# An attention decode kernel: a third P buffer with K units mixed into value stages, no dummy transposes, and the last QK of a phase at once

## The chip, the cores and the metric

The kernel runs on one core of one Trainium2 chip. The metric is device time in microseconds of that core. PE is the matrix engine, DVE the vector engine, ACT the scalar engine, SP the engine that here issues all loads. "Granted clock" is the share of PE's full clock that the throttle let through; 0.50 is half speed.

Ratios are the mean time of one kernel's fast runs over the mean of the fast runs of the kernel before in the same rounds on the same chip, so a ratio is not quite the quotient of the medians quoted. A stage length is one execution's.

## The reference, cut to what matters

Two layers, each attention with a KV cache and then a gated feed-forward block, applied twice to four rows (B = 4) of one token each. Both attention layers read the same caches.

```
q = (layernorm(x) @ wq)                     # 32 heads of 128, 8 KV heads: 4 query heads share one
scores = q @ k_cache^T * 128**-0.5          # k_cache, v_cache: (4 rows, 8 groups, 8192, 128), bf16
o = softmax(scores) @ v_cache
x = x + o @ wo
x = x + (silu(layernorm(x) @ w_gate) * (layernorm(x) @ w_up)) @ w_down
# the same once more
```

K and V of one row are 33.6 MB. The kernel keeps eleven value pieces of 512 KB of a row on the chip from the first layer to the second; the rest of the caches is read twice.

## The kernel before

The work is cut into units of 2048 cache positions of one group, 512 KB each. A K unit transposes its 16 blocks on PE, copies them out of PSUM, the memory that PE writes (DVE or ACT), and multiplies with the query (QK). After the eight groups of a chunk comes the softmax; after the fourth chunk a finalization that rescales P and transposes it. A value unit is 16 narrow matmuls of P against V. Between value units the kernel before issues dummy transposes, whose results nothing reads; the function is called `warm`.

```
NRING = 7; NRET = 11; NKT = 6          # load ring, kept value buffers, transposed-K buffers
pp = sb("pp", [P, 2, S // NJ], BF16)   # P of two rows (layer, row) -> row % 2
...
phases = [("A1", 0, A_of(0, 0, range(NCH)))]                       # K of row 0, layer 1
for b in range(B):
    ...                                                             # B1: values of row b, layer 1,
    phases.append(("B1", b, mine))                                  #     merged with K of row b+1; 5 values at the end
    phases.append(("C1", b, fill))                                  # C1: feed-forward + 11 value units of row b+1
    phases.append(("A2", b, merge(A_of(1, b, range(NCH)), mid) + tail))   # A2: K of row b, layer 2
    phases.append(("B2", b, B_of(1, b, gs_)))                       # B2: values of row b, layer 2, alone
...
def do(u):
    if u[0] == "k":
        hv = k_front(u)                           # transposes and copies
        prev, pending[:] = list(pending), [(u, hv)]
        for x in prev:
            k_back(*x)                            # QK of the K unit before this one
    else:
        v_unit(u)
        if last_kind[0] == "v":
            warm(warmth["n"])                     # 8 dummy transposes (4 in C1)
    last_kind[0] = u[0]
    run_delayed()
    pump()                                        # next loads, as ring buffers come free
...
elif name == "B1":
    some(len(units)); flush(); settle()           # the last QK only here, after the value tail
```

I call C1 the feed-forward stage, A2 the second-layer K stage, B2 the second-layer value stage. The last B2 also contains the final feed-forward and the output.

## Time and profile before

| | before |
|---|---|
| time, median (3 runs) | 759.7 us (758.5 to 761.5) |
| profiled span | 764.7 us |
| PE busy / DVE / ACT | 87% / 42% / 31% |
| loads | 259.3 MB, mean 341 GB/s with all packets |

From the page of the kernel before: engines, clock and transfer rate in 40 slices of 19.1 us, the DMA account, the chain that ended last, and two groups of instructions (line, engine, operation, operands, count; then busy us and mean ns of one; then idle time before them).

```profile
span 764.7 us, 28617 instructions
PE 668.4 (87%) x13048; PEld 516.8 (68%) x13048; DVE 324.5 (42%) x727; ACT 235.2 (31%) x304; POOL 0.7 (0%) x6
PEclk9989788995799999996599999997599996699898
GB/s 354 388 390 407 367 404 378 410 409 238 262 402 407 334 278 407 408 408 261 237 381 405 367 288 352 409 408 325 239 337 407 349 328 281 258 406 356 295 256 62
DMA packets 75129, 261.13 MB, mean 341 GB/s; under 512 B 7672, under 2 KB 13568, under 8 KB 74496
PE 62%; DMA 25%; DVE 5%; issue 3%; ACT 3%; SPq 2%; ACTq 0%
L384 PE MATMUL ps<-ident,ring 128*128 128x128 bf16 x4096 | 286.6, 226 | 26.4 <-DMA ring<-in_A_k_cache_dram 26.1
L518 PE MATMUL ps<-ident 128*128 128x128 bf16 x1440 | 129.4, 236 | 0.8 <-issue 0.6
```

The best slices move 407 to 410 GB/s. PE seems the fuller engine, but line 518 are the dummies: 129.4 us of its 668.4. The Trainium skill ("Perfetto Trace Analysis", opening note) says that matmul busy time is a bad metric of nearness to the limit; its reason is that matmuls are pipelined. Here there is another: a fifth of the busy time computes nothing.

The windows view gives one stage per line: from:to, length, busy time of each engine, then granted clock, DMA share and GB/s. I cut within 0.3 us of the first matmul of each stage's first unit. In order: feed-forward of row 0, value stage of row 0, feed-forward of row 1, value stage of row 1, last value stage and output.

```profile
176.40:198.80 22.40, 22.40 (x552) 19.03 (x553) 4.72 (x25) 1.26 (x5) 0.00 (x0) 0.50 0.66 217
255.90:287.40 31.50, 29.76 (x785) 22.76 (x782) 3.85 (x15) 0.00 (x0) 0.00 (x0) 1.00 0.86 293
352.60:375.60 23.00, 22.51 (x553) 19.08 (x553) 4.72 (x25) 1.26 (x5) 0.00 (x0) 0.50 0.66 213
433.50:467.40 33.90, 30.93 (x788) 23.77 (x785) 3.88 (x15) 0.00 (x0) 0.00 (x0) 0.95 0.89 301
720.00:764.70 44.70, 39.22 (x1083) 31.88 (x1082) 7.45 (x33) 0.75 (x3) 0.00 (x0) 0.93 0.56 189
```

The feed-forward stages have PE full at half clock and the queue at 213 to 217 GB/s. The value stages have PE full at full clock (with dummies) and the queue at 293 to 301.

### The profile page before, as it was taken

How to read it: one execution, taken by the hardware profiler on the slowest of the kernel's cores; microseconds unless marked ns; L12 is line 12 of the kernel's file. 1: busy time of each engine (PE TensorE's matmuls, PEld its weight loads, DVE VectorE, ACT ScalarE, POOL GpSimd, SP SyncE). 2: the span in 40 equal slices, each digit the busy share in tenths (PEclk: the TensorE clock that was granted, in tenths of full speed). 3: DMA queues.
4: the chain of work that ended last, by engine and by line, in shares of the span. 5: the costliest groups of instructions: out<-in, count | busy, mean ns of one | idle time of the engine just before them, and what ended most of it. 6: DMA issues, size and time to landing. Idle time of an engine off the chain costs nothing.

```text
span 764.7 us, 28617 instructions
## 1 busy us (share of the span) xinstructions
PE 668.4 (87%) x13048; PEld 516.8 (68%) x13048; DVE 324.5 (42%) x727; ACT 235.2 (31%) x304; POOL 0.7 (0%) x6
## 2 busy tenths in 40 slices
PE   3888678778999998997999999997999899999797
PEld 3655556557876776666877667665877677876576
DVE  2545444433366215544266413653266511366312
ACT  0544233321265004541156102551056300156100
POOL 0000000000000000000000000000000000000000
PEclk9989788995799999996599999997599996699898
DMA  8999999996899989997799989998799887899872
GB/s 354 388 390 407 367 404 378 410 409 238 262 402 407 334 278 407 408 408 261 237 381 405 367 288 352 409 408 325 239 337 407 349 328 281 258 406 356 295 256 62
DMA packets 75129, 261.13 MB, mean 341 GB/s; under 512 B 7672, under 2 KB 13568, under 8 KB 74496
## 3 DMA queue, kind: packets, MB, share of 16 engines
q1 hardware_dynamic: 75008, 259.30, 90.4%
q8 instruction: 102, 1.67, 0.9%
q14 instruction: 19, 0.16, 0.1%
HBM read 259.26 MB, written 0.00 MB: 339 GB/s over the span
## 4 chain that ended last, share of the span: by engine, by line
PE 62%; DMA 25%; DVE 5%; issue 3%; ACT 3%; SPq 2%; ACTq 0%
PE ps L384 22%; DMA ring<-in_A_k_cache_dram 18%; PE ps L518 14%; PE ps L497 10%; PE ps L400 6%; DMA ring<-in_A_v_cache_dram 6%; PE ps L580 2%; SPq L92 2%; PE ps L599 2%; DMA wq_sb<-in_A_wq_dram 2%; PE ps L540 2%; DVE negm L412 1%; ACT ktp L250 1%; PE ps L635 1%; ACT pp L414 1%
## 5 line engine op out<-in xcount | busy, mean ns | idle before, releaser
L384 PE MATMUL ps<-ident,ring 128*128 128x128 bf16 x4096 | 286.6, 226 | 26.4 <-DMA ring<-in_A_k_cache_dram 26.1
L384 PEld LDWEIGHTS ps<-ident,ring 128*128 128x128 bf16 x4096 | 242.8, 101 | 77.8 <-DMA ring<-in_A_k_cache_dram 45.2
L248 DVE COPY ktp<-ps 128x1024 bf16<-128x1024 bf16 x320 | 215.2, 689 | 178.3 <-PE ps L384 177.1
L250 ACT ACTIVATE ktp<-ps 128x1024 bf16<-128x1024 bf16 x192 | 195.1, 1022 | 293.7 <-PE ps L384 293.7
L518 PE MATMUL ps<-ident 128*128 128x128 bf16 x1440 | 129.4, 236 | 0.8 <-issue 0.6
L400 PE MATMUL ps<-ktp,qpad 128*32 128x512 bf16 x1024 | 110.7, 398 | 2.8 <-ACT ktp L250 2.4
L518 PEld LDWEIGHTS ps<-ident 128*128 128x128 bf16 x1440 | 89.4, 104 | 27.5 <-issue 11.6
L497 PE MATMUL ps<-ring,pp 128*32 128x128 bf16 x2688 | 82.3, 251 | 9.7 <-issue 5.0
L506 DVE TENSOR_SCALAR o_g<-ps,wrow 128x128 bf16<-128x128 f32 x64 | 22.4, 349 | 142.3 <-PE ps L497 142.3
L497 PEld LDWEIGHTS ps<-ring,pp 128*32 128x32 bf16 x2688 | 48.7, 107 | 25.7 <-issue 10.3
L400 PEld LDWEIGHTS ps<-ktp,qpad 128*32 128x32 bf16 x1024 | 27.9, 93 | 35.8 <-ACT ktp L250 6.3
L573 ACT ACTIVATE lnv<-var,eps_sb 128x4 f32<-128x4 f32 x10 | 3.0, 298 | 156.4 <-DVE var L560 156.4
L497 PE MATMUL ps<-kept,pp 128*32 128x128 bf16 x1408 | 36.7, 223 | 6.3 <-DMA kept<-in_A_v_cache_dram 4.4
L414 ACT ACTIVATE pp<-ps,negm 128x512 bf16<-128x512 f32 x32 | 22.0, 687 | 44.9 <-DVE negm L412 42.7
L497 PEld LDWEIGHTS ps<-kept,pp 128*32 128x32 bf16 x1408 | 22.0, 96 | 14.0 <-DMA kept<-in_A_v_cache_dram 6.5
L412 DVE TENSOR_REDUCE negm<-ps 128x1 f32<-128x512 f32 x32 | 22.1, 690 | 7.7 <-PE ps L400 6.0
L580 PE MATMUL ps<-xnT,wq_sb 128*128 128x4 bf16 x640 | 17.9, 166 | 8.3 <-DMA wq_sb<-in_A_wq_dram 7.8
L540 PEld LDWEIGHTS ps<-oT,wo_sb 128*128 128x128 bf16 x640 | 20.2, 99 | 7.0 <-issue 4.2
L540 PE MATMUL ps<-oT,wo_sb 128*128 128x4 bf16 x640 | 22.2, 165 | 2.5 <-DVE oT L528 1.3
L580 PEld LDWEIGHTS ps<-xnT,wq_sb 128*128 128x128 bf16 x640 | 17.6, 104 | 8.5 <-DMA wq_sb<-in_A_wq_dram 7.9
L447 PE MATMUL ps<-ident,pp 128*128 128x128 bf16 x128 | 10.9, 244 | 10.6 <-DVE pp L431 10.6
L525 PE MATMUL ps<-selh,o_g 128*128 128x4 bf16 x64 | 11.6, 180 | 9.0 <-DVE o_g L506 8.6
(76 smaller groups left out, 195.4 us busy)
## 6 DMA issues: line engine op xcount, KB each, us to landing
ring<-in_A_k_cache_dram SPq DMA_DIRECT2D x256, 512.0 KB, 7.2
ring<-in_A_v_cache_dram SPq DMA_DIRECT2D x168, 512.0 KB, 6.8
kept<-in_A_v_cache_dram SPq DMA_DIRECT2D x44, 512.0 KB, 9.9
wq_sb<-in_A_wq_dram SPq DMA_DIRECT2D x1, 4096.0 KB, 12.5
wo_sb<-in_A_wo_dram SPq DMA_DIRECT2D x4, 1024.0 KB, 12.0
wg_sb<-in_B_w_gate_dram SPq DMA_DIRECT2D x2, 896.0 KB, 12.0
wu_sb<-in_B_w_up_dram SPq DMA_DIRECT2D x2, 896.0 KB, 11.9
wd_sb<-in_B_w_down_dram SPq DMA_DIRECT2D x2, 896.0 KB, 9.3
```

What stands on the lines that cost most here:

```text
L92: ins = self.eng[engname].dma_start(out_ap, in_ap)
L248: T.op("dve", lambda e: e.tensor_copy(dst, src), reads=reads, writes=writes)
L250: T.op("act", lambda e: e.activation(dst, src, ACTF.Copy), reads=reads, writes=writes)
L384: T.op("pe", lambda e: e.matmul(stg[:, t * P:(t + 1) * P], lhsT=ap[:, blk * Dh:(blk + 1) * Dh], rhs=ident[:], is_transpose=True, start=Tru ...
L400: T.op("pe", lambda e: e.matmul(ps[32 * j:32 * (j + 1), bk * BW:(bk + 1) * BW], lhsT=qp, rhs=ktp[:, s, (j % 2) * 512:(j % 2 + 1) * 512], s ...
L412: T.op("dve", lambda e: e.tensor_reduce(negm[:, q, c:c + 1], bank(bk), AX.X, ALU.max, negate=True), reads=[f"pb{bk}"], writes=[f"negm{q}_{ ...
L414: T.op("act", lambda e: e.activation(pp[:, q, c * 512:(c + 1) * 512], bank(bk), ACTF.Exp, bias=negm[:, q, c:c + 1], scale=1.0, accum_out=l ...
L497: T.op("pe", lambda e: e.matmul(ps[32 * j:32 * (j + 1), bk * BW:bk * BW + Dh], lhsT=pp[:, q, (c * NM + m) * P + 32 * j:(c * NM + m) * P + ...
L506: T.op("dve", lambda e: e.tensor_scalar(o_g[:, og, :], ps[:, bk * BW:bk * BW + Dh], wrow[:, q:q + 1], None, op0=ALU.mult), reads=[f"pb{bk} ...
L518: T.op("pe", lambda e: e.matmul(stg[:, 0:P], lhsT=ident[:], rhs=ident[:], is_transpose=True, start=True, stop=True), reads=["ident"], writ ...
L540: T.op("pe", lambda e: e.matmul(ps[:, OPJ * BW + nq * B:OPJ * BW + (nq + 1) * B], lhsT=wo_sb[:, h, nq * P:(nq + 1) * P], rhs=oT[:, l, h, : ...
L580: T.op("pe", lambda e: e.matmul(misc[:, h * B:(h + 1) * B], lhsT=wq_sb[:, kt, h * Dh:(h + 1) * Dh], rhs=xnT[:, kt * B:(kt + 1) * B], start ...
```

## The change

Its intent: with P buffers for three rows, the K units of the next-but-one row can run in the second-layer value stage, where they bring loads into stretches that only use kept values. Value units are redistributed over feed-forward and K stages. The dummy transposes go. The last QK of a first-layer phase is issued at once, as that of a second-layer phase was before, so that the softmax and the transposes of P run behind the value units at the end of the phase. To pay for the third P buffer, six transposed-K buffers become four. The core of the diff (the code for alternating PSUM banks, `ALT`, is added but switched off):

```diff
-    NKT = 6
+    NKT = 4
...
-        pp = sb("pp", [P, 2, S // NJ], BF16)
+        pp = sb("pp", [P, 3, S // NJ], BF16)
...
+        TAIL1 = [16, 7, 8]
+        TAIL2 = [3, 4, 3, 4]
+        NFILL = [10, 13, 14, 9]
+        LATE = [8, 8, 16]
...
+            v2, late = split(B_of(1, b, V2O[b]), (LATE + [0])[b])
+            if b + 1 < B:
+                v2 = v2 + B_of(0, b + 1, V1O[b + 1][5:])
+            if b + 2 < B:
+                early = B_of(0, b + 2, V1O[b + 2][:5])
+                head, tail = split(v2, TAIL1[b + 1])
+                v2 = head[:LEAD[b]] + mix(A_of(0, b + 2, range(NCH)), head[LEAD[b]:]) + tail
...
-            pbuf[(0, b)] = b % 2
-            pbuf[(1, b)] = b % 2
+            pbuf[(0, b)] = b % 3
+            pbuf[(1, b)] = b % 3
...
             if u[0] == "k":
                 hv = k_front(u)
-                prev, pending[:] = list(pending), [(u, hv)]
-                for x in prev:
-                    k_back(*x)
+                if not hold["on"]:
+                    flush()
+                pending.append((u, hv))
+                if u[3] == G - 1 and u[4] == NCH - 1:
+                    flush()
             else:
                 v_unit(u)
-                if last_kind[0] == "v":
-                    warm(warmth["n"])
...
```

More of the change, by code (lines that the diff above doesn't have):

```diff
@@ L167, in bass_interleave_layers__gqa_block_cached__swiglu_ffn__decode_kernel @@
         xnT = sb("xnT", [P, NQ * B], BF16)
-        negm = sb("negm", [P, 2, NCH], FP32)
-        lsum = sb("lsum", [P, 2, NCH], FP32)
-        gm = sb("gm", [P, 2, 2], FP32)
+        negm = sb("negm", [P, 3, NCH], FP32)
+        lsum = sb("lsum", [P, 3, NCH], FP32)
+        gm = sb("gm", [P, 3, 2], FP32)
         dm = sb("dm", [P, NCH], FP32)
-        alpha = sb("alpha", [P, 2, NCH], FP32)
+        alpha = sb("alpha", [P, 3, NCH], FP32)
         wl = sb("wl", [P, NCH], FP32)
@@ L178, in bass_interleave_layers__gqa_block_cached__swiglu_ffn__decode_kernel @@
         one1 = sb("one1", [1, 1], FP32)
-        wrow = sb("wrow", [P, 2], FP32)
+        wrow = sb("wrow", [P, 3], FP32)
         o_g = sb("o_g", [P, 2, Dh], BF16)
@@ L198, in bass_interleave_layers__gqa_block_cached__swiglu_ffn__decode_kernel @@
         SBANK = (3, 4)
+        PVALT = 2
         OPJ = 6
@@ L230, in bass_interleave_layers__gqa_block_cached__swiglu_ffn__decode_kernel @@
         nc.scalar.preload_act_table_set("natural_log_exp_and_others")
-        tbanks = {"list": [0, 1, 2], "n": 0}
+        tbanks = {"n": 0}
+        pvb = {"k": 5, "alt": False}
         def next_bank():
-            L = tbanks["list"]
+            L = [0, 1] if pvb["alt"] or pvb["k"] == PVALT else [0, 1, 2]
             k = L[tbanks["n"] % len(L)]
@@ L263, in bass_interleave_layers__gqa_block_cached__swiglu_ffn__decode_kernel, with mix @@
                     kept_ix[(g, c)] = len(kept_ix)
-        def merge(a, b):
+        def mix(a, b):
+            if len(a) < len(b):
+                a, b = b, a
             n, m = len(a), len(b)
-            if m == 0:
-                return list(a)
-            r, i, k = [], 0, 0
-            for x in a:
+            r, k = [], 0
+            for i, x in enumerate(a):
                 r.append(x)
-                i += 1
-                while k < m and (k + 1) * n <= i * m:
+                while k < m and (k + 1) * n <= (i + 1) * m:
                     r.append(b[k])
@@ L279, in bass_interleave_layers__gqa_block_cached__swiglu_ffn__decode_kernel @@
         B_of = lambda l, b, gs: sum((VU(l, b, g) for g in gs), [])
-        REST = [0, 1, 2]
-        EARLY = [3, 4, 5, 6, 7]
-        LATE = [4, 5, 6, 7]
+        TAIL1 = [16, 7, 8]
+        TAIL2 = [3, 4, 3, 4]
+        NFILL = [10, 13, 14, 9]
+        LATE = [8, 8, 16]
+        LEAD = [2, 2]
+        ECUT = [0, 0, 0, 0]
+        FL = [1, 2, 1, 1, 2, 1, 2, 2]
+        V1O = [[3, 4, 5, 6, 7, 0, 1, 2]] * 4
+        V2O = [[3, 0, 4, 1, 5, 2, 6, 7], [3, 4, 0, 1, 5, 2, 6, 7], [3, 0, 1, 2, 5, 4, 6, 7], [0, 3, 4, 1, 5, 2, 6, 7]]
+        ALT = ()
         def split(us, n):
@@ L287, in bass_interleave_layers__gqa_block_cached__swiglu_ffn__decode_kernel @@
         phases = [("A1", 0, A_of(0, 0, range(NCH)))]
-        for b in range(B):
-            nxt = b + 1 < B
-            mine = B_of(0, b, EARLY + REST if b == 0 else REST)
-            if nxt:
-                head, tail = split(mine, 5)
-                ahead = A_of(0, b + 1, range(NCH))
-                mine = (merge(ahead, head) if len(ahead) > len(head) else merge(head, ahead)) + tail
-            phases.append(("B1", b, mine))
-            light = B_of(0, b + 1, EARLY) if nxt else B_of(1, b - 1, LATE)
-            fill, more = light[:11], light[11:]
-            phases.append(("C1", b, fill))
-            mid, tail = split(more, 5)
-            phases.append(("A2", b, merge(A_of(1, b, range(NCH)), mid) + tail))
-            gs_ = [3, 0, 4, 1, 5, 2, 6, 7] if b != B - 2 else [3, 0, 1, 2]
-            phases.append(("B2", b, B_of(1, b, gs_)))
+        ahead = B_of(0, 0, V1O[0])
+        head, tail = split(ahead, TAIL1[0])
+        phases.append(("B1", 0, mix(A_of(0, 1, range(NCH)), head) + tail))
+        early = B_of(0, 1, V1O[1][:5])
+        late = []
+        for b in range(B):
+            fill = early[:ECUT[b]] + late + early[ECUT[b]:]
+            fill, more = fill[:NFILL[b]], fill[NFILL[b]:]
+            phases.append(("C1", b, fill))
+            mid, tail = split(more, min(len(more), TAIL2[b]))
+            phases.append(("A2", b, mix(A_of(1, b, range(NCH)), mid) + tail))
+            v2, late = split(B_of(1, b, V2O[b]), (LATE + [0])[b])
[5 more added lines that the diff above has]
+                v2 = head[:LEAD[b]] + mix(A_of(0, b + 2, range(NCH)), head[LEAD[b]:]) + tail
+            else:
+                early = []
+            phases.append(("B2", b, v2))
         order = [u for _, _, us in phases for u in us]
+        assert len(set(order)) == len(order) == 4 * B * G * NCH
         loads = []
@@ L485, in row_spread @@
                  reads=[f"pb{bk2}"], writes=[f"wrow{q}"])
-        pvb = {"k": 5}
         def v_unit(u):
@@ L493, in v_unit @@
             ap, key = home[u]
+            if c == 0:
+                pvb["k"] = PVALT if pvb["alt"] and pvb["k"] == 5 else 5
             bk = pvb["k"]
@@ L504, in v_unit @@
             if c == NCH - 1:
+                pvb["k"] = 5 if not pvb["alt"] else pvb["k"]
                 og = g % 2
@@ L512, in v_unit @@
                     delayed.append((1, run_oproj))
-        def warm(n):
-            bk = next_bank()
-            stg = bank_bf(bk)
-            for t in range(n):
-                T.op("pe", lambda e: e.matmul(stg[:, 0:P], lhsT=ident[:], rhs=ident[:], is_transpose=True,
-                                              start=True, stop=True),
-                     reads=["ident"], writes=[f"pb{bk}"], sig=(t == n - 1))
         def o_select(l, b, g):
@@ L671, in do @@
                 hv = k_front(u)
-                prev, pending[:] = list(pending), [(u, hv)]
-                for x in prev:
-                    k_back(*x)
+                if not hold["on"]:
[3 more added lines that the diff above has]
+                    flush()
             else:
                 v_unit(u)
-                if last_kind[0] == "v":
-                    warm(warmth["n"])
-            last_kind[0] = u[0]
             run_delayed()
@@ L686, in flush @@
             pending.clear()
-        warmth = {"n": 8}
-        last_kind = [None]
+        hold = {"on": False}
         def settle():
@@ L696, in bass_interleave_layers__gqa_block_cached__swiglu_ffn__decode_kernel @@
         for name, b, units in phases:
-            warmth["n"] = 4 if name == "C1" else 8
+            pvb["alt"] = name in ALT
             it = iter(units)
@@ L709, in bass_interleave_layers__gqa_block_cached__swiglu_ffn__decode_kernel @@
                 some(len(units))
-                flush()
                 settle()
@@ L713, in bass_interleave_layers__gqa_block_cached__swiglu_ffn__decode_kernel @@
                 some(len(units))
-                flush()
                 settle()
@@ L718, in bass_interleave_layers__gqa_block_cached__swiglu_ffn__decode_kernel @@
                 op_state["open"] = False
+                hold["on"] = True
                 add_to_x(x0T, "x0", OPJ)
-                some(1)
+                some(FL[0])
                 ln_center()
-                some(1)
+                some(FL[1])
                 ffn_gate()
                 ln_scale()
-                some(1)
+                some(FL[2])
                 ffn_gate_act()
                 ffn_up()
-                some(1)
+                some(FL[3])
                 ffn_up_act()
-                some(2)
+                some(FL[4])
                 ffn_down()
                 add_to_x(XT, "x", MISC)
-                some(1)
+                some(FL[5])
                 ln_center()
-                some(1)
+                some(FL[6])
                 q_proj()
@@ L739, in bass_interleave_layers__gqa_block_cached__swiglu_ffn__decode_kernel @@
                 q_fill(qpad2, "qpad2", b, 0)
+                some(FL[7])
+                hold["on"] = False
+                flush()
                 some(len(units))
@@ L744, in bass_interleave_layers__gqa_block_cached__swiglu_ffn__decode_kernel @@
             elif name == "A2":
-                for u in units:
-                    do(u)
-                    if u == ("k", 1, b, G - 1, NCH - 1):
-                        flush()
-                flush()
+                some(len(units))
                 settle()
```

## The prediction

> **What bounds the kernel now.** The DMA queue, or stages that leave it empty. The page's DMA part has 259.3 MB through the one load queue; the best slices, and a 30 us window inside a mixed stretch, run at 408 GB/s, so loads alone need 259.3 MB / 408 GB/s = 636 us of the profiled 764.7. (The Trainium skill, "DMA: Bandwidth & Descriptors", Specifications, puts the fabric at 435 GB/s; the best slice here shows 410.) The missing 129 us lie where the seven ring buffers come free too slowly. Cutting the span at each stage's first unit (windows view):
>
> - four feed-forward stages, 21.5 to 23.0 us each, 216 to 235 GB/s: about 10 us of transfer lost in each, 40 in all;
> - value-only second-layer stages, 31.5 and 33.8 us (294 and 302 GB/s) and 15.0 us: 24 lost;
> - second-layer K stages, 56 to 58 us, 346 to 379 GB/s: 22 lost;
> - last value stage and output, 42.9 us at 195 GB/s: 22 lost;
> - start and first-layer stages (386 to 400 GB/s): about 15.
>
> PE looks full (87% busy), but 129 us of that are the 1440 dummy transposes. A K unit repeats every 1.33 us at full clock; a value unit takes 0.33 to 0.41, 0.62 at half clock. Per row that is 64 x 1.33 + 64 x 0.4 + about 17 = 128 us, against 117 loads x 1.285 us = 150 us of DMA: PE has slack on average, unevenly spread.
>
> **What changes.** The third P buffer lets the next-but-one row's 32 K units run in the second-layer value stage, between units whose kept values need no load. That stage then wants 57 loads (73 us) for 32 x 1.33 + 36 x 0.4 = 57 us of PE: DMA-bound instead of starved. Eight to 16 second-layer value units move into the next feed-forward and K stages. Dropping the dummies saves about 0.45 us for each of some 10 value units in a feed-forward stage (pitch with dummies 1.09, value alone 0.62), so 22 us becomes about 17.5, while 9 to 14 ring buffers come free (12 to 18 us of DMA). The last stage's pitch falls from 0.89-0.98 to DMA pace. Four transposed-K buffers instead of six should cost nothing: two units' halves are alive at a time. The last QK at once saves below 1.5 us per phase.
>
> **Sum (estimate from the above).** 636 us of transfer, plus idle: feed-forward 13, second-layer K stages 14, mixed stages 9, start and first stage 4, from last landing to output 12, slack 5: 693 of profiled span; timed runs are some 5 us shorter: 688 us. Range 672 to 710. Chances: faster 0.96, same 0.03, slower 0.01.
>
> **What would show it.** DMA mean up from 341 to about 375 GB/s; slices of 240-290 GB/s mostly gone; feed-forward stages near 18 us, over 280 GB/s in the middle two; second-layer value stages with K above 385 GB/s; PE busy down by more than 100 us, its waits on ring DMA up from 26 us; chain of waits more than half DMA.
>
> **What would make it wrong.** Without dummies the granted clock may fall to half in DMA-bound mixes (the Trainium skill, "TensorE: Matmul & The Clock Gate", Part 1, says idle windows halve it; here it is 0.50 in feed-forward stages, 0.88 in the first mix). A K unit at half clock takes about 2.4 us, above its load's 1.285, so a mix could turn PE-bound: 700 to 720. Blocking of the one queue by kept buffers would do the same.

## More of the kernel before

A value group ends with DVE scaling the output (`o_g`), a small matmul that selects heads (`o_select`), and 16 matmuls of the output projection where the row or layer is due.

PE's waits (waiting line, released by: us in total, times, longest):

```profile
PE ps L384 <- DMA ring<-in_A_k_cache_dram: 26.1, 34, 2.4
PE ps L525 <- DVE o_g L506: 8.6, 12, 3.2
PE ps L447 <- DVE pp L431: 10.6, 7, 2.1
PE ps L497 <- issue: 6.9, 8, 1.9
```

## The result, and the profile after

The changed kernel took 712.05 us in the median (710.08 to 713.17, 4 runs) against 760.6 us, a ratio of 0.936 (95% interval 0.933 to 0.939). On other chips it took 713.6, 716.4 and 714.8 us (ratios 0.938, 0.944, 0.940). It is faster by 6%, and 24 us above the predicted 688.

The same parts of the page of the changed kernel (its line 399 is line 384 of before):

```profile
span 710.2 us, 25752 instructions
PE 565.1 (80%) x11608; PEld 438.1 (62%) x11608; DVE 324.1 (46%) x727; ACT 236.0 (33%) x304; POOL 0.7 (0%) x6
PEclk9999899985599999975799899985699975599855
GB/s 351 388 387 407 373 399 408 407 408 405 257 395 408 395 380 403 401 407 343 288 411 408 384 382 392 376 408 368 268 412 407 407 293 410 236 377 381 347 353 66
DMA packets 75118, 260.95 MB, mean 367 GB/s; under 512 B 7672, under 2 KB 13568, under 8 KB 74496
PE 47%; DMA 36%; DVE 7%; issue 4%; ACT 3%; SPq 2%; ACTq 0%; DVEq 0%
L399 PE MATMUL ps<-ident,ring 128*128 128x128 bf16 x4096 | 286.7, 226 | 40.5 <-DMA ring<-in_A_k_cache_dram 40.1
```

PE lost 103 us of busy time, the queue's mean rose from 341 to 367 GB/s, but there are still five slices below 295 GB/s besides the last. The windows view of the four feed-forward stages and the last stage:

```profile
168.90:188.40 19.50, 16.73 (x500) 14.73 (x497) 4.42 (x22) 0.92 (x4) 0.00 (x0) 0.50 0.96 361
320.00:343.50 23.50, 18.16 (x536) 15.86 (x533) 5.17 (x26) 1.25 (x5) 0.00 (x0) 0.50 0.81 302
484.00:507.80 23.80, 18.84 (x550) 16.20 (x548) 5.17 (x26) 1.25 (x5) 0.00 (x0) 0.50 0.84 299
594.70:614.20 19.50, 15.76 (x463) 13.66 (x461) 4.15 (x21) 0.75 (x3) 0.00 (x0) 0.50 0.93 355
670.50:710.20 39.70, 28.82 (x825) 23.37 (x825) 7.39 (x32) 0.75 (x3) 0.00 (x0) 0.50 0.59 216
```

The two middle feed-forward stages are no shorter than before (23.5 and 23.8 us against 23.0 and 22.4), though they move more. The last stage, 39.7 against 44.7 us, runs at half clock throughout. PE is busy 28.8 us of it, and the stage moves 216 GB/s: the queue isn't its limit. PE's waits:

```profile
PE ps L399 <- DMA ring<-in_A_k_cache_dram: 40.1, 52, 2.8
PE ps L533 <- DVE o_g L522: 28.9, 57, 1.2
PE ps L462 <- DVE pp L446: 15.0, 8, 2.1
PE ps L588 <- issue: 5.7, 3, 2.5
PE ps L512 <- issue: 7.0, 7, 1.7
```

PE now waits 28.9 us for the scaled output (line 533 after DVE's `o_g`), which the dummies used to cover (8.6 us), and there are waits called "issue" (the profile shows nothing that PE waited for) in stages where nothing but the program itself should hold PE. One of them, from the timeline of PE in the second feed-forward stage (start, length, what, idle before it):

```profile
334.39 2.91 PE L588 MATMUL ps<-xnT,wq_sb 128*128 128x4 bf16 x103
339.81 0.80 PE L588 MATMUL ps<-xnT,wq_sb 128*128 128x4 bf16 x25 [2.52 <-issue]
```

A run of 128 equal matmuls stops in its middle for 2.52 us; nothing in the program stands there. The trace's packets of the instruction queue (91 of 16 KB each, for PE's 23,216 matmuls and weight loads) tell more. I listed every pause of over 0.45 us from start to start inside a run of matmuls of one line, where the next instruction waits for no semaphore, beside the end of the last instruction packet before it:

```
changed kernel: restart at us, pause us, us since the last instruction packet ended
181.45  2.04  1.22      493.16  1.38  1.45      606.15  1.10  1.44      689.30  0.97  1.40
328.79  1.35  1.35      504.19  2.35  1.51      612.09  1.19  1.37      695.24  0.85  1.35
339.81  2.68  1.49      600.75  1.10  1.39      683.09  1.44  1.56
```

All 11, and all 9 in the kernel before, restart 1.2 to 1.6 us after such a packet. All 11 lie in the feed-forward stages and the last stage.

Where the 70.6 us lie that separate the span from its transfers (261.0 MB at 408 GB/s = 639.6 us), each stage's length less its own bytes at 408 GB/s:

| idle of the load queue, us | before | predicted | after |
|---|---|---|---|
| four feed-forward stages | 41 | 13 | 18 |
| second-layer K stages | 22 | 14 | 18 |
| value stages, first-layer and mixed | 34 | 9 | 12 |
| start and first stage | 4 | 4 | 4 |
| last stage and output | 24 | 12 | 19 |
| slack | | 5 | |
| sum (rounded after adding) | 125 | 57 | 71 |

### The profile page after: what moved, and what is told of

Its sections match the earlier page's. It is cut to its first block, busy times and chain, and to the rows that moved or that the text cites. A ratio compares the mean times of both kernels' runs of the same rounds, so it can differ in the third digit from the quotient of the medians.

```text
span 710.2 us, 25752 instructions
## 1 busy us (share of the span) xinstructions
PE 565.1 (80%) x11608; PEld 438.1 (62%) x11608; DVE 324.1 (46%) x727; ACT 236.0 (33%) x304; POOL 0.7 (0%) x6
## 4 chain that ended last, share of the span: by engine, by line
PE 47%; DMA 36%; DVE 7%; issue 4%; ACT 3%; SPq 2%; ACTq 0%; DVEq 0%
DMA ring<-in_A_k_cache_dram 29%; PE ps L399 22%; PE ps L512 8%; PE ps L415 6%; DMA ring<-in_A_v_cache_dram 5%; PE ps L588 3%; SPq L92 2%; PE ps L607 2%; DMA wq_sb<-in_A_wq_dram 2%; PE ps L548 2%; DVE o_g L522 2%; PE ps L643 1%; ACT ktp L252 1%; DVE negm L427 1%; PE ps L565 1%
## 5 line engine op out<-in xcount | busy, mean ns | idle before, releaser
L512 PEld LDWEIGHTS ps<-ring,pp 128*32 128x32 bf16 x2688 | 56.2, 114 | 20.5 <-issue 7.6
L512 PE MATMUL ps<-kept,pp 128*32 128x128 bf16 x1408 | 42.0, 266 | 9.1 <-DMA kept<-in_A_v_cache_dram 6.9
L512 PEld LDWEIGHTS ps<-kept,pp 128*32 128x32 bf16 x1408 | 29.5, 116 | 16.5 <-DMA kept<-in_A_v_cache_dram 10.4
L533 PE MATMUL ps<-selh,o_g 128*128 128x4 bf16 x64 | 11.7, 183 | 29.2 <-DVE o_g L522 28.9
L533 PEld LDWEIGHTS ps<-selh,o_g 128*128 128x128 bf16 x64 | 6.4, 101 | 42.1 <-DVE o_g L522 42.0
L427 DVE TENSOR_REDUCE negm<-ps 128x1 f32<-128x512 f32 x32 | 22.1, 690 | 11.1 <-PE ps L415 9.5
L588 PEld LDWEIGHTS ps<-xnT,wq_sb 128*128 128x128 bf16 x640 | 17.7, 104 | 14.7 <-DMA wq_sb<-in_A_wq_dram 8.0
L462 PEld LDWEIGHTS ps<-ident,pp 128*128 128x128 bf16 x128 | 7.9, 103 | 17.3 <-DVE pp L446 16.5
```

The costliest lines, as they stand in the source:

```text
L427: T.op("dve", lambda e: e.tensor_reduce(negm[:, q, c:c + 1], bank(bk), AX.X, ALU.max, negate=True), reads=[f"pb{bk}"], writes=[f"negm{q}_{ ...
L462: T.op("pe", lambda e: e.matmul(stg[:, t * P:(t + 1) * P], lhsT=pp[:, q, blk * P:(blk + 1) * P], rhs=ident[:], is_transpose=True, start=Tr ...
L512: T.op("pe", lambda e: e.matmul(ps[32 * j:32 * (j + 1), bk * BW:bk * BW + Dh], lhsT=pp[:, q, (c * NM + m) * P + 32 * j:(c * NM + m) * P + ...
L533: T.op("pe", lambda e: e.matmul(ps[:, bk * BW:bk * BW + REP], lhsT=o_g[:, og, :], rhs=selh[:, g * REP:(g + 1) * REP], start=True, stop=Tru ...
L588: T.op("pe", lambda e: e.matmul(misc[:, h * B:(h + 1) * B], lhsT=wq_sb[:, kt, h * Dh:(h + 1) * Dh], rhs=xnT[:, kt * B:(kt + 1) * B], start ...
```

## Experiments

Each edit is against the kernel that its heading names.

### Dummies alone, in both orders

`before_nodummy` is the kernel before with

```diff
-                if last_kind[0] == "v":
-                    warm(warmth["n"])
```

> The old order and two P buffers, dummy transposes removed alone. Theory A (the dummies cost PE time where the DMA queue starves): feed-forward stages fall from 22.4 us to 17 to 18 us, the value-only second-layer stages by 5 us, the last stage by 5 us, in all 20 to 28 us: about 735 us; the mean granted clock falls from 0.89. Theory B (the dummies hold the clock, so without them units run at half clock and nothing is gained): 755 us or more.

Measured: 727.9 us against 758.7, ratio 0.959 (0.955 to 0.963). This is more than theory A asked for in all; B falls. Where A put the gain is only partly right: the feed-forward stages fell to 20.7, 19.8, 20.5 and 19.4 us, not to 17 to 18, and the value-only stages and the last stage gained more than the 5 us each that A gave them. The two value-only stages of the second layer, which the mix was to cure, in the windows view:

```profile
252.70:277.80 25.10, 15.85 (x530) 12.05 (x527) 3.99 (x15) 0.00 (x0) 0.00 (x0) 0.64 1.01 393
419.70:445.00 25.30, 16.54 (x530) 12.71 (x527) 3.98 (x15) 0.00 (x0) 0.00 (x0) 0.63 0.99 387
```

With the dummies gone they take 25 us instead of 31.5 and 33.9, and move 387 to 393 GB/s, though the clock falls to 0.64. They were starved by the dummies, not by a lack of loads to do.

`after_dummy` puts the dummies back into the changed kernel by the old rule:

```diff
...
                 v_unit(u)
+                if last_kind[0] == "v":
+                    warm(warmth["n"])
...
```

> The changed kernel with the dummy transposes of before put back by the old rule (8 after a value unit that follows a value unit, 4 in feed-forward stages). Theory A: feed-forward stages and the last stage are 4 to 5 us longer each, partly absorbed by stages where the DMA queue is the limit: 724 to 735 us. Theory B: the clock is back at 0.89 or more and the time is 712 us or less.

Measured: 739.0 us, ratio 0.974 (0.970 to 0.978), on the same chip as the run above. This is above A's range; B falls again (the mean clock is back at 0.91, the time is not). The last stage took 45.5 us at clock 0.89 (to the last compute instruction), against 37.9 in the changed kernel. The feed-forward stages, which A wanted 4 to 5 us longer, hardly changed in sum (87.8 us against 86.3): the first mixed stage, the value-only stage of row 2 and the last stage grew by some 7 us each.

### The last QK at once

`after_lateqk` undoes it in the changed kernel:

```diff
-                if u[3] == G - 1 and u[4] == NCH - 1:
+                if u[3] == G - 1 and u[4] == NCH - 1 and u[1] == 1:
                     flush()
...
             elif name == "B1":
                 some(len(units))
+                flush()
                 settle()                # the same in A1 and in B2
```

> The changed kernel with the last QK of the first layer's K units issued at the end of the phase again, as before, not at once. Theory E (the prediction's: worth below 1.5 us per phase): at most 6 us slower than the changed kernel. Theory F (softmax and the transposes of P, some 8 us, now hide behind the 7 to 16 value units of the tail and would stand bare after it): 10 to 25 us slower, with PE idle before the transposes of P and before the row weights up by as much.

Measured: 730.6 us against 713.6 for `after_same`, the changed kernel: 17 us. F's size holds; its signs are looked at below. The first-layer value stage of row 0 and the second-layer value stage of row 0 in the windows view, the changed kernel first, then with the late QK:

```profile
81.40:168.40 87.00, 67.03 (x1305) 51.01 (x1305) 38.21 (x77) 28.88 (x35) 0.00 (x0) 0.85 1.02 401
247.80:323.30 75.50, 62.38 (x1299) 47.64 (x1297) 38.65 (x79) 27.63 (x34) 0.00 (x0) 0.91 1.01 389
```

```profile
81.30:175.50 94.20, 68.69 (x1310) 50.86 (x1309) 38.24 (x76) 28.88 (x35) 0.00 (x0) 0.81 0.99 390
254.00:334.20 80.20, 62.67 (x1305) 47.55 (x1302) 38.64 (x78) 27.74 (x34) 0.00 (x0) 0.88 0.99 384
```

They are 7.2 and 4.7 us longer (and the one of row 1 by 5.8), with nearly the same PE work. That is where F put the loss. What F said of PE's waits did not show as waits: those for the transposes of P and for the row weights hardly moved (15.0 to 14.7 and 13.0 to 15.3 us), while those for kept value loads rose from 6.4 to 13.7. Their sum does not account for 17 us. PE waits for this chain in both kernels; what differs is what stands between its steps, and the timeline shows that. With the late QK, 8.0, 8.2 and 8.0 us pass in the three stages from the last QK to the next value unit, and no value unit runs in between that would free a ring buffer. The load queue runs dry. In the windows view, the chain at the end of the first of these stages: the changed kernel, then the late QK and the stretch after it.

```profile
145.50:154.00 8.50, 4.72 (x104) 3.73 (x102) 5.28 (x18) 2.72 (x6) 0.00 (x0) 0.80 1.03 407
```

```profile
167.70:175.70 8.00, 3.96 (x42) 2.92 (x41) 5.11 (x17) 2.20 (x5) 0.00 (x0) 0.50 0.67 268
175.70:182.00 6.30, 5.83 (x165) 5.10 (x165) 1.93 (x12) 0.75 (x3) 0.00 (x0) 0.50 0.69 204
```

The changed kernel moves 407 GB/s while the same chain runs among value units; with the late QK it is 268, and 204 after it. So F's mechanism, the chain standing bare, is seen; its sign, longer waits of PE, was the wrong one.

> The changed kernel again, as the yardstick for the other kernels of this call on the same chip: 709 to 716 us, ratio 0.93 to 0.945.

`after_same` came as expected: 713.6 us, 0.938 (0.935 to 0.942).

`before_qk` makes the same step alone in the kernel before (a `flush()` after the last K unit in `do`).

> The old order with its dummy transposes; only the last QK of the first layer's K units is issued at once. Undoing it in the changed kernel cost 17 us. If it is worth as much wherever a tail of value units follows (three tails of 5 units here): 8 to 15 us below before, 745 to 752 us. If the tail of 5 units is too short to hide the softmax behind: within 4 us of before.

Measured: 770.3 us, ratio 1.014 (1.008 to 1.019): both expectations missed. It is slower by an interval clear of 1. PE's waits only changed place: for the row weights 11.0 to 2.6 us, for the scaled P 10.6 to 15.5, for the copied output 1.3 to 9.1. In this version the delayed transposes of P also come one unit earlier in the second-layer K stages, since the flush now precedes the countdown. Why it loses 10 us on balance is not settled.

### Everything but the third buffer and the order

`before_nodummy_qk` has both edits: no dummies and the early `flush()`.

> The old order and two P buffers, no dummies, last QK at once: everything of the change but the third buffer and the new order. Theory I (the mix fills value-only stages, as predicted: 24 us were lost in them): 715 us or more above what the changed kernel takes, that is 725 to 732 us against some 713. Theory J (without dummies these stages already run at 387 to 393 GB/s, so the mix has nothing left to fill): within 6 us of the changed kernel.

Measured: 722.1 us, ratio 0.951 (0.945 to 0.956), beside `after_again`, the changed kernel, 716.4 us, 0.944 (0.939 to 0.948).

> The changed kernel once more, as the yardstick of this call's chip: 709 to 717 us.

The difference is 5.7 us, just inside J's limit, and the intervals overlap: the third buffer and the new order, for which the change is named, are worth 0 to 2%. Without the early QK they are worth nothing that these runs show: `after_lateqk` 0.960 against `before_nodummy` 0.959 (different chips).

### Four transposed-K buffers

`before_nkt4` is the kernel before with `NKT = 4`.

> The kernel before with four transposed-K buffers instead of six and nothing else. The prediction's reading (two units' halves are alive at a time): within 3 us of before. Rival (the copies wait for QK): PE's waits for the copied K up from 2.4 us, 5 us or more slower.

Measured: 759.2 us, ratio 0.999 (0.993 to 1.004). PE's wait for the copied K is the same 2.4 us. The shrink is free, as predicted.

### What the room of the third buffer buys elsewhere

`ring8` takes the old order with two P buffers:

```diff
-    NRING = 7
+    NRING = 8
-    NKT = 6
+    NKT = 4
...                                    # no dummies, early flush, as in before_nodummy_qk
```

> The old order with two P buffers, no dummies, last QK at once, four transposed-K buffers, and the 8 KB that this frees against the changed kernel's third P buffer spent on an eighth ring buffer (4 KB). If depth of the ring is what the feed-forward and second-layer K stages lack, each stage gets one load more: 5 to 10 us below before_nodummy_qk's 722, 712 to 717 us, level with the changed kernel or better. If the new order matters more than depth: 719 us or more.

Measured: 717.7 us, ratio 0.943 (0.939 to 0.946), beside `after_third`, the changed kernel, 714.8 us, 0.940 (0.937 to 0.943). (The room is 4 KB per partition, not 8 as the text says.) The time falls between the two ranges that were set. The two kernels cannot be told apart by these runs, so the old order with an eighth ring buffer is no worse choice than the third P buffer and the new order. What the eighth buffer adds to `before_nodummy_qk` (0.951, 0.945 to 0.956, on another chip) is not shown either: those intervals overlap too.

> The changed kernel, as the yardstick on this chip: ratio 0.936 to 0.944.

### The wait for the scaled output

`after_hide` issues the selection one unit later, everywhere, and alternates PSUM banks where no K unit runs:

```diff
-                delayed.append((0, lambda: o_select(l, b, g)))
+                delayed.append((1, lambda: o_select(l, b, g)))
-                    delayed.append((1, lambda: opq.append((l, g))))
-                    delayed.append((1, run_oproj))
+                    delayed.append((2, lambda: opq.append((l, g))))
+                    delayed.append((2, run_oproj))
-            pvb["alt"] = name in ALT
+            pvb["alt"] = name == "C1" or (name == "B2" and b >= B - 2)
```

> The changed kernel with the output selection of a group issued one unit later, so that PE does not wait for the scaled output, and with value groups alternating between two PSUM banks in the feed-forward stages and the last two value stages. Theory C (PE's wait of 28.9 us for the scaled output is on the critical path only where no DMA is waited for: feed-forward and last stage): that wait falls under 5 us, last stage from 37.9 to about 33 us, feed-forward stages 1 us shorter each: 703 to 706 us. Rival D (the DMA queue hides it everywhere): within 2 us of the changed kernel.

Measured: 716.1 us, ratio 0.942 (0.938 to 0.946): no gain (the changed kernel had 0.936 to 0.944). The wait for the scaled output did fall, from 28.9 to 5.5 us, but others took its place: ring loads 40 to 50 us, the copied output 2 to 11. The last stage was 37.1 us instead of 37.9, and the pauses inside matmul runs were 19.2 us in sum against 16.5 in the first trace of the changed kernel (and 13.8 to 17.3 in its later ones).

`after_hide2` uses the later selection only in the feed-forward stages and the last two value stages; `after_late5` is the same kernel again.

> As after_hide, but the later output selection is used only in the feed-forward stages and the last two value stages. If PE's wait for the scaled output is what makes these stages long, the time is 3 to 6 us below the changed kernel's on the same chip. If they are paced by the arrival of PE's instructions (every stall of over 0.45 us inside a run of matmuls ended 1.2 to 1.6 us after a packet of the instruction queue), the time is within 2 us of it, and the stalls grow by what the wait lost.

> after_hide2 again with five rounds: its ratio was 0.9351 against 0.9383 for the changed kernel, intervals overlapping. If the gain is real: 1.5 to 4 us below after_third with intervals apart; if not, within 1.5 us.

Measured: 711.4 us (0.935, 0.933 to 0.938) against 713.6 (0.938) on one chip, and 711.2 us (0.936, 0.933 to 0.940) against 714.8 (0.940) on another. Both times 2 to 4 us faster, both times with overlapping intervals, so a gain is not shown. The second feed-forward stage went from 23.4 to 20.7 us; pauses grew from 13.8 to 17.9 us; and the K stage after the first feed-forward went from 59.6 to 61.3.

`ring8_late` is the same edit on `ring8`.

> ring8 with the output selection one unit later in the feed-forward and last two value stages. If the wait for the scaled output lengthens these stages: 3 to 6 us below ring8. If instruction packets pace them: within 2 us of ring8.

Measured: 734.4 us, ratio 0.966: 17 us slower, which neither view had foreseen. The last K stage grew from 55.5 to 65.6 us. A reading from the program: in this order the alternation leaves an unfinished value group in PSUM bank 2 all through that stage, and while it does, the K transposes have two banks instead of three. No run tests this in `ring8_late` itself.

`after_late_b5` tests that reading in the changed kernel: no alternation in the first feed-forward stage, so that the unfinished group holds bank 5. Against `after_late5`:

```diff
-            pvb["alt"] = pvb["late"] = name == "C1" or (name == "B2" and b >= B - 2)
+            pvb["late"] = name == "C1" or (name == "B2" and b >= B - 2)
+            pvb["alt"] = pvb["late"] and (name, b) != ("C1", 0)
```

> after_late5 without alternating banks in the first feed-forward stage, so that the value group that is left unfinished there holds bank 5 and not one of the three banks that the K transposes use. If the held bank is what made the next K stage 61 to 62 us: that stage is back at 58 to 60 us and the total is 708 to 711 us, a ratio of 0.931 to 0.936, below the changed kernel's 0.936 to 0.944. If not: the stage stays above 61 us and the ratio at 0.936 or more.

Measured: the K stage is back at 57.3 us (61.3 and 62.2 with the bank held, 57.8 to 60.0 in the four profiles of the changed kernel), as the bank reading says. The total is 710.6 us, the lowest median of all, but the ratio, 0.938 (0.935 to 0.940), is above the range that I had set: this chip's kernel before was fast too (759.0). It is not shown to beat the changed kernel.

### Half clock and late instructions

`after_fill` gives the last stage eight dummies per value group, at the place where PE waits for the scaled output:

```diff
             if c == NCH - 1:
...
+                if l == 1 and b == B - 1:
+                    warm(8)
                 delayed.append((0, lambda: o_select(l, b, g)))
```

> The changed kernel with 8 dummy transposes at the end of each value group of the last stage only, where PE waits for the scaled output anyway. If 8 per group hold the clock: granted clock of the last stage rises from 0.50 to above 0.8, a group takes about 2.3 us instead of 3.1, last stage 37.9 to about 32 us, total 706 us. If not: clock stays 0.50, the dummies take 0.86 us against a wait of 0.46, and the total is 714 to 716 us.

Measured: 718.5 us, ratio 0.946 (0.942 to 0.949). The clock rose to 0.70, and yet the stage did not become shorter: 40.2 us to the last compute instruction, against 37.0 to 39.3 in the four profiles of the changed kernel. Its pauses summed to 8.3 us, one of them 3.58, against 1.9 to 4.4. Less the pauses, it is 31.9 us against 34.6 to 35.2. Neither expectation fits: the clock came back, and the late instructions took what it gave.

`probe_noload` (wrong result) lets the value units of the feed-forward stages and the last stage read kept buffers, so that these stages load nothing:

```diff
...                                    # quiet: the units of the feed-forward stages and of the last stage
+            probe = u in quiet and (g, c) not in kept_ix
+            if probe:
+                s = n % NRET
+                home[u] = (kept[:, s, :], f"kept{s}")
-            if kind == "v" and (g, c) in kept_ix:
+            elif kind == "v" and (g, c) in kept_ix:
```

> Wrong result on purpose: in the feed-forward stages and the last value stage, value units that should read a freshly loaded buffer read a kept one, so these stages load nothing. Theory G (instruction packets come late because the same DMA engines are full of loads): the stalls inside runs of matmuls vanish there, the second and third feed-forward stages fall from 23.5 to about 20 us, the last stage from 37.9 to 33 us or less. Rival H (the instruction stream is too slow whatever the loads do): stalls of 1 to 2.7 us remain and feed-forward stages stay within 1.5 us of 23.5. The total falls in any case, by some 65 loads of 1.285 us.

Two of the feed-forward stages and the last stage:

```profile
320.00:339.70 19.70, 17.77 (x537) 15.72 (x535) 5.18 (x26) 1.26 (x5) 0.00 (x0) 0.50 0.24 91
499.10:518.60 19.50, 17.96 (x549) 15.96 (x546) 5.18 (x26) 1.25 (x5) 0.00 (x0) 0.50 0.09 29
690.40:726.50 36.10, 27.79 (x825) 23.33 (x825) 7.36 (x32) 0.75 (x3) 0.00 (x0) 0.50 0.01 3
```

Pauses in matmul runs fell from 10 (13.8 us in `after_same`, the same chip) to 2 (1.3 us, one of them outside these stages). The four feed-forward stages took 17.3, 19.6, 19.5 and 15.8 us against 19.8, 23.4, 22.1 and 18.9 in `after_same`: 3 us less each on the mean. Less its own pauses, each of these stages of `after_same` (17.5, 19.4, 19.5 and 16.1 us) is within 0.3 us of its length in the probe, so the pauses are the whole difference. H falls: PE's instructions come late because of the loads. G's reason, that the loads fill the DMA engines, is not shown: the instruction packets of these stages took as long with loads (0.88 to 1.21 us) as without (0.91 to 1.45), so what delays them lies before their start, where the trace shows nothing. The last stage, to the last compute instruction, is still 34.3 us (37.0 in `after_same`): G's 33 is not quite reached, and most of that stage is PE's own time at half clock. The total did not fall as I had written (728.3 us): the probe frees kept buffers too early, and PE waits 34 us for kept loads, nearly all of it in two second-layer value stages and 21.6 us of it at once. So only its stages count.

`probe_fill` is the same with the dummies of `after_fill`.

> Wrong result on purpose: probe_noload with 8 dummy transposes at the end of each value group of the last stage, as in after_fill. If the half clock is what makes the last stage long once nothing is loaded: the clock there rises from 0.50 to 0.7 or more and the stage falls from 34.3 to about 29 us, without a stall over 0.45 us inside a run of matmuls; with loads the same dummies made it 40.2 us. If the clock doesn't matter: 34 us or more.

The last stage of `after_fill`, with loads, and then of `probe_fill`, without:

```profile
675.40:717.40 42.00, 29.82 (x889) 25.52 (x889) 7.39 (x32) 0.75 (x3) 0.00 (x0) 0.70 0.57 207
```

```profile
689.70:721.70 32.00, 26.84 (x889) 23.11 (x889) 7.43 (x32) 0.75 (x3) 0.00 (x0) 0.77 0.01 4
```

The same PE instructions take 42.0 us with loads and 32.0 without (40.2 and 30.2 to the last compute instruction). So the half clock costs at least 4.1 us of the unloaded stage (34.3 to 30.2, at clock 0.77 and with one pause of 0.57; expected were 0.70 or more, about 29 us and no pause), and with loads the faster clock brought nothing, since the instructions did not arrive in time.

## Why the prediction was wrong

The direction and the rough mechanism were right; the time was 712 against 688, just outside the range. In the prediction's own words:

- **"timed runs are some 5 us shorter"** was wrong, and with the last stage the largest miss: 7 of the 24 us. It compared one profiled execution of the kernel before (766.6 us, at the slow end) with the median of others. A run's time is its span plus 1.7 to 2.6 us here, 1.8 in the changed kernel's.
- **"feed-forward 13"** measured 18. The step that failed is "so 22 us becomes about 17.5": the stages took 19.5, 23.5, 23.8 and 19.5 us. I had counted PE's work and the freed buffers, and left out that the loads which now run there delay PE's instructions; without loads they are 3 us shorter (`probe_noload`). The rest is that the middle two hold 13 and 14 value units, not "some 10": the stage with ten took 17.3 us without loads, so PE's own work had been sized rightly.
- **"from last landing to output 12"** measured 19. The step that failed is "The last stage's pitch falls from 0.89-0.98 to DMA pace". The stage is bound by PE: 34.3 us remain without any load. Value matmuls alone ran at clock 0.50 there, and each group adds the wait for the scaled output and 16 projection matmuls.
- **"636 us of transfer"** left out 1.7 MB of instructions: 4 us. **"Second-layer K stages 14"** measured 18, 8.6 of them in the last one, which has the fewest value units to mix in. **"Mixed stages 9"** measured 12, 4.4 of it in the value stage of row 2, which has no K units left to mix in. The slack of 5 covers a part of these misses. The sum is off by 17 us, the span was 710.2 against 693.
- **"DMA-bound instead of starved"**: the text credits this to the third P buffer. `before_nodummy` shows 387 to 393 GB/s there without any third buffer. The dummies had starved it. Their removal alone is worth 31 us of the 44 to 49; with the early QK it is 38; order and third buffer add about 6, with intervals that overlap. So the order's gain was not lost on the chip: most of it had another source, and that this term of the sum came out near was luck.
- **"The last QK at once saves below 1.5 us per phase"** was wrong the other way: undoing it costs 17 us in the new order, because there 7 to 16 value units stand behind it and the chain that it starts takes 8 us, bare or not. Alone in the kernel before it cost 1.4%, for a reason that stays open.
- **"Four transposed-K buffers ... should cost nothing"**: right (0.999).
- **The feared half clock in mixes** did not decide it: the mixes run at 0.87 to 0.93 and 391 to 399 GB/s. It fell to half where no one was waiting for the queue: in the last stage, from 0.93 to 0.50. That 712 lies in the 700 to 720 written down for half-clock mixes is chance.

Of the signs: mean rate 367, not 375; slow slices halved, not gone; second-layer value stages with K at 391 and 398, as said; PE busy down by 103 us and waits on ring loads up from 26 to 40, as said; the chain 36% DMA, not over half.

## What to carry to other kernels

Before a new schedule is built to fill a starved stage, take away what fills the engine there without computing: the dummies that held the clock cost more than the half clock they prevented. Where a long chain (softmax, transposes) ends a phase, start it before the filler work and not after it, and check that there is enough filler: with five value units behind it (`before_qk`) the same step did not pay here. In a stage of very short matmuls, count instructions as well as time: beside saturated loads PE waited for its own program, and adding instructions to use up a wait did not shorten the stage, though it raised the clock.

## What the Trainium skill lacked or had wrong

- "TensorE: Matmul & The Clock Gate", Part 4, says of transposes that the full clock doesn't engage for transpose-mode. Here it does: value units with eight dummy transposes each ran at granted clock 1.00 and 0.95, the same units without them at 0.64 and 0.63, and in the last stage at 0.93 with them and 0.51 without.
- The same page, Part 1, has activity release the throttle and idle windows bring it back. In the feed-forward stage of row 0, PE was busy 22.40 of 22.40 us by the records and held at 0.50. The page does not say that PE can be busy throughout, by the records, and stay at half clock. The work there was matmuls of 4 columns, value matmuls with 32-column weights and four dummies per value unit; which of these fails to count as activity no run separates.
- "Runtime: NRT & Kernel Launch", Instruction fetch mechanics, has blocks of 16 KiB, 256 instructions, which the trace shows (91 packets of 16,384 bytes), and calls the cost of crossing a block "mostly hidden". In stages that load 216 to 361 GB/s it is not: 11 pauses of 0.85 to 2.68 us, 16.5 us in all, each ending 1.2 to 1.6 us after such a packet, against 2 pauses (1.3 us) in the whole run when those stages loaded nothing.
